# Products of blocks 1 to 3 over 64 rows in two orders of tiles, single maxima between them, first weights by GpSimd's queue

## The chip, the cores and the metric

The kernel runs on one core of a Trainium2 chip. The metric is the device time of one execution in microseconds; times of several executions are given by their median. The engines are TensorE (PE; PEld is its weight load), VectorE (DVE), ScalarE (ACT), GpSimd (POOL) and SyncE (SP), which here only issues DMA transfers. All tensors are float32.

## What is computed

The reference, cut to what matters (S = 2048 tokens, D = 640, 32 heads of width 20, one shared head of keys and values):

```python
a = x @ dft_hid_re.T;  b = x @ dft_hid_im.T
A = dft_seq_re @ a - dft_seq_im @ b            # Fourier mixing
q = (x @ wq) per head;  k = x @ wk;  v = x @ wv
p = softmax(q @ k.T * 20 ** -0.5)
B = (p @ v) of all heads @ wo
g = sigmoid((x * gate_w).sum(-1, keepdims=True))
out = g * A + (1 - g) * B
```

Every float32 factor of a product is split into a high part and a low part of type float32r, and a product is three products: high by high, high by low and low by high.

## The kernel before, in words

One long function writes the instructions of PE, ACT, DVE and POOL in the order in which they run; SP's transfers are ordered by the framework's planner, after what they depend on. It has four stages, and only the first three are touched by the change.

**Block 0** (lines 435 to 461). x is taken in four blocks of 512 tokens, each in five chunks c of 128 of the 640 features. For chunk c, `load_x1` fetches x, `move` fetches the rows of `wq`, `split_x1` and `split` make high and low parts (high on ACT, low on DVE), and PE multiplies: `kv_mm` (L397, two matmuls for keys, values and gate together, whose weights `kvg` are 41 columns wide) and, for the five tiles m of 128 columns of q, `q_mm` with its three matmuls (L119 to L121). Each tile has a PSUM bank of its own. Nine matmuls on an identity (L103) run ahead, to fill the time until data arrive. When a tile is complete, `q_out` copies its high part (ACT, L387) and low part (DVE, L388) out of PSUM into `qh` and `ql`, of which there are three buffers each, and stores both in DRAM. `kv_out` (L405 to L411) adds the two halves of the keys, splits them and copies them into six strips of `ks` by DMAs from POOL's queue; `kv_turn` (L417) transposes keys, values and gate by four small matmuls.

**Blocks 1 to 3** (lines 464 to 500). The same tiles one after the other, all five chunks of a tile in a row, with matmuls over all 128 rows of the array: 85 a block. Between the q tiles stand the first *maxima*: for a head and 128 queries the scores against 512 keys are computed on PE in a matmul over 60 rows (`a_unit`, L248; head 0 of a pair on rows 0 to 63, head 1 on rows 64 to 127) and reduced to their maximum on DVE (L255). A *unit* is both heads. They come in groups of four matmuls (two units), 13 groups in all: after tiles 2 to 4 of block 1 and after each tile of blocks 2 and 3, in the banks S1 to S4. Unit 4 is the first that reads queries of block 1, units 8, 16 and 24 the first that read keys of blocks 1, 2 and 3. The queries that the maxima read lie in `qs`, with high, high and low part of a head in three strips; `load_qs0` loads the first pair of heads from DRAM, half by half.

**The lead** (lines 1101 to 1123). 120 steps of the first product of the Fourier mixing (`y_put`, L793): each step is a pair of matmuls over 64 rows, one on the upper and one on the lower half of the array, into two banks that `lrot` hands out and that ACT evicts every 15 steps (L830). Between them the maxima go on until 80 halves are done, from step `LATE` on, in the banks S2 to S4; with unit 31 a pair of heads is complete. Then `a_reduce` to `a_final` (L258 to L278) form the maxima's rows, which SP stores to `m_d` and loads into two rows of `qs` at delays counted by `tick`. Four score matmuls of the second kind (`b_unit`, L973, over 62 rows, with ACT's exponential, L981), which need those rows, are placed by `EARLY_B` in bank V.

**The loop** (from line 1125). Hand-written plans of maxima, scores, exponentials, value products and Fourier products until the end.

## Time and profile before

| what | us |
|---|---|
| median of 3 runs | 1717.25 (1717.0 to 1718.81) |
| the profiled execution's own time | 1717.17 |
| its span, first to last instruction | 1715.4 |
| granted TensorE clock | 1.000 |

The profile is one execution. Its page gives busy times, the chain that ended last and groups of instructions; the timeline gives instructions in order of time, as "start, duration, engine, line, operation, out<-in, shape, count", with the idle time before and what ended it in brackets. A duration of a matmul covers its whole pipeline; the distance of starts is what it takes from the array. Where several equal instructions follow one another, a row merges them and its duration covers all ("x4").

### The profile page before, as it was taken

How to read it: one execution, taken by the hardware profiler on the slowest of the kernel's cores; microseconds unless marked ns; L12 is line 12 of the kernel's file. 1: busy time of each engine (PE TensorE's matmuls, PEld its weight loads, DVE VectorE, ACT ScalarE, POOL GpSimd, SP SyncE). 2: the span in 40 equal slices, each digit the busy share in tenths (PEclk: the TensorE clock that was granted, in tenths of full speed). 3: DMA queues.
4: the chain of work that ended last, by engine and by line, in shares of the span. 5: the costliest groups of instructions: out<-in, count | busy, mean ns of one | idle time of the engine just before them, and what ended most of it. 6: DMA issues, size and time to landing. Idle time of an engine off the chain costs nothing.

```text
span 1715.4 us, 43386 instructions
## 1 busy us (share of the span) xinstructions
PE 1705.8 (99%) x16766; PEld 1235.5 (72%) x16766; DVE 1378.8 (80%) x2295; ACT 1251.3 (73%) x2547; POOL 1116.0 (65%) x944
## 2 busy tenths in 40 slices
PE   9999999999999999999999999999999999999998
PEld 7687677777777777777777777777777777777665
DVE  5889888888888888888888888888888888888823
ACT  4247788888876777777777777777777767678897
POOL 2355556332366568758767888888887765547787
PEclk9999999999999999999999999999999999999999
DMA  8641223222264546546666776665555533143332
GB/s 283 190 138 52 76 76 105 76 79 72 80 224 160 190 155 209 160 147 215 224 216 203 236 233 224 203 185 186 176 176 165 160 111 117 52 123 112 113 91 99
DMA packets 180538, 261.47 MB, mean 152 GB/s; under 512 B 35872, under 2 KB 134688, under 8 KB 180332
## 3 DMA queue, kind: packets, MB, share of 16 engines
q1 hardware_dynamic: 179420, 257.55, 47.0%
q8 instruction: 132, 2.16, 0.5%
q0 software_dynamic: 768, 0.99, 0.3%
q14 instruction: 74, 0.61, 0.1%
q10 hardware_dynamic: 144, 0.16, 0.0%
HBM read 184.42 MB, written 76.99 MB: 152 GB/s over the span
## 4 chain that ended last, share of the span: by engine, by line
PE 98%; ACT 1%; DMA 0%; issue 0%; DVE 0%; POOL 0%; SPq 0%; DVEq 0%; ACTq 0%
PE av L985 27%; PE y_p L793 21%; PE b L973 19%; PE a L248 15%; PE ab L793 7%; PE oo L793 3%; PE q L119 1%; PE q L121 1%; PE q L120 1%; PE kv L397 1%; ACT pt L981 0%; DMA wraw<-in_wq_dram 0%; PE o L119 0%; PE o L121 0%; PE o L120 0%
## 5 line engine op out<-in xcount | busy, mean ns | idle before, releaser
L255 DVE TENSOR_REDUCE mx<-a 128x1 f32<-128x512 f32 x2048 | 1304.0, 686 | 242.9 <-PE a L248 203.3
L981 ACT ACTIVATE pt<-b 128x512 f32<-128x512 f32 x2048 | 1058.3, 624 | 345.6 <-PE a L248 267.6
L973 PE MATMUL b<-qs,ks 62*128 62x512 f32 x2048 | 758.2, 408 | 1.9 <-ACT pt L981 1.4
L248 PE MATMUL a<-ks,qs 60*128 60x512 f32 x2048 | 704.3, 407 | 0.4 <-DVE mx L255 0.4
L793 PE MATMUL y_p<-tb,ch 64*128 64x320 f32 x3584 | 618.5, 307 | 0.0
L793 PEld LDWEIGHTS y_p<-tb,ch 64*128 64x128 f32 x3584 | 504.7, 186 | 3.0
L985 PE MATMUL av<-pt,vsb 128*32 128x512 f32 x4096 | 484.9, 597 | 0.0
L973 PEld LDWEIGHTS b<-qs,ks 62*128 62x128 f32 x2048 | 346.2, 184 | 185.9 <-DVE mx L255 125.2
L793 PE MATMUL y_p<-tb,cl 64*128 64x320 f32 x1792 | 455.2, 306 | 0.0
L248 PEld LDWEIGHTS a<-ks,qs 60*128 60x128 f32 x2048 | 345.7, 185 | 13.1 <-issue 2.2
L793 PEld LDWEIGHTS y_p<-tb,cl 64*128 64x128 f32 x1792 | 296.5, 185 | 3.1
L985 PEld LDWEIGHTS av<-pt,vsb 128*32 128x32 f32 x4096 | 111.4, 109 | 240.2 <-issue 230.2
L548 POOL TENSOR_TENSOR cl<-craw,ch 128x1024 fp32r<-128x1024 f32 x112 | 268.3, 2395 | 9.0
L835 POOL TENSOR_TENSOR yt<-yt,yu 128x320 f32<-128x320 f32 x86 | 75.7, 881 | 293.5 <-ACT yu L830 260.3
L835 POOL TENSOR_TENSOR abt<-abt,abu 128x320 f32<-128x320 f32 x64 | 55.7, 870 | 193.8 <-ACT abu L830 172.8
L542 POOL TENSOR_TENSOR craw<-craw 128x1024 f32<-128x1024 f32 x64 | 153.3, 2395 | 0.0
L547 POOL CAST ch<-craw 128x1024 fp32r<-128x1024 f32 x112 | 116.4, 1039 | 6.4 <-PE ab L793 2.2
L793 PE MATMUL oo<-wo,osp 64*128 64x320 f32 x816 | 91.4, 306 | 0.0
L793 PEld LDWEIGHTS oo<-wo,osp 64*128 64x128 f32 x816 | 86.5, 185 | 1.6
L574 POOL TENSOR_TENSOR tb<-braw,tb 128x320 fp32r<-128x320 f32 x80 | 69.6, 875 | 0.0
L793 PE MATMUL ab<-wbh,xh 64*128 64x320 f32 x256 | 60.1, 307 | 0.0
L793 PE MATMUL ab<-wbh,xl 64*128 64x320 f32 x256 | 59.6, 305 | 0.0
(142 smaller groups left out, 1619.2 us busy)
## 6 DMA issues: line engine op xcount, KB each, us to landing
craw<-in_cre_dram SPq DMA_DIRECT2D x80, 512.0 KB
craw<-in_cim_dram SPq DMA_DIRECT2D x64, 512.0 KB
s_d<-craw SPq DMA_DIRECT2D x32, 512.0 KB
craw<-s_d SPq DMA_DIRECT2D x32, 512.0 KB
braw<-b_d SPq DMA_DIRECT2D x80, 160.0 KB
xraw<-in_xT_dram SPq DMA_DIRECT2D x32, 320.0 KB
b_d<-abt SPq DMA_DIRECT2D x64, 160.0 KB
t_d<-braw SPq DMA_DIRECT2D x64, 160.0 KB
```

Source lines behind the costliest of these rows:

```text
L119: nc.tensor.matmul(ps, wh, xh, start=(i == 0), stop=False)
L248: nc.tensor.matmul(ps, qs[v][b : b + 60, qb * P : (qb + 1) * P], ks[b : b + 60, c * ROW : (c + 1) * ROW], start=True, stop=True,)
L255: nc.vector.tensor_reduce(mx[v][:, hh, qb, c : c + 1], ps, axis=AX.X, op=ALU.max)
L542: nc.gpsimd.tensor_tensor(x, raw[0], x, op=how)
L547: nc.gpsimd.tensor_copy(h, x)
L548: nc.gpsimd.tensor_tensor(l, x, h.bitcast(F32), op=ALU.subtract)
L574: nc.gpsimd.tensor_tensor(t[:, 1], raw, t[:, 0].bitcast(F32), op=ALU.subtract)
L793: nc.tensor.matmul(ps, w, x, start=start, stop=stop)
L835: nc.gpsimd.tensor_tensor(t0, t0, t1, op=ALU.add)
L973: nc.tensor.matmul(ps, ks[b : b + 62, kc * P : (kc + 1) * P], qs[NPAIR * (qc // 2) + p][b : b + 62, (qc % 2) * ROW : (qc % 2 + 1) * ROW], ...
L981: nc.scalar.activation(t, ps, AF.Exp, scale=SCALE)
L985: nc.tensor.matmul(ps[32 * g : 32 * g + 32, :], vsb[:, kc, :], t, start=first, stop=last)
```

## The change

In blocks 1 to 3 every product over 128 rows becomes two over 64, on the upper and the lower half of the array. A new class `Tile` holds a tile's list of matmuls, takes its bank when first run, and runs the list once on each half, into the same bank. The two halves go through a block's six tiles in different orders, (kv, 1, 0, 2, 3, 4) and (0, kv, 3, 4, 1, 2), so that they are never at the same tile at one time; the second pass over a tile begins with the matmul that ended the first (its list runs backwards there), and between the passes ACT copies one column of that matmul's weights onto itself, which orders the second pass behind the first. Five banks serve these tiles. Maxima stand singly in each half's order, 30 in each, every seven matmuls from 40 on and every six from 220 on (counted over the three blocks), the lower half's four matmuls later, in the banks S2 to S4. Loads, splits and transposes are tied to positions of that count.

Block 0 keeps full matmuls, but in chunk 0 the order is changed, the products for keys and values come a chunk later, and q's tiles end one after the other. The first chunk of `wq` comes in two pieces of 256 and 384 columns by POOL's queue; `kvg` is fetched and split after chunk 1. Low parts of x from block 1 on are made by POOL. `q_out` fills the first pair of heads of `qs` from SBUF by six DMAs of POOL's queue for blocks 0 and 1, and `load_qs0` goes. In the lead, `lrot` gives other banks (the last group sits in V and F1), maxima start at step 4 rather than 8 and are 20 halves rather than 28, the four b halves stand at steps 64 to 94 rather than 102 to 117, and the maxima's rows are stored at once and loaded a tick later. One warming matmul less is made.

```diff
-    for _ in range(9):
+    for _ in range(8):
...
     def later(n, f, *args):
-        todo.append((clock["n"] + n, f, args))
+        if n < 0:
+            f(*args)
+        else:
+            todo.append((clock["n"] + n, f, args))
...
-            later(1, move, m_d[v][i].rearrange("r g t -> g r t"), m3[:, 1 + i])
+            later(1 if stage["loop"] else -1, move, m_d[v][i].rearrange("r g t -> g r t"), m3[:, 1 + i])
...
-            later(5 if stage["loop"] else 3, move, qs[v][r : r + 2], ...
+            later(5 if stage["loop"] else 1, move, qs[v][r : r + 2], ...
...
+        pieces = (slice(0, 2 * P), slice(2 * P, D))
+        raw0 = w1.tile([P, D], F32, name="wraw", bufs=2)
+        for cs in pieces:
+            nc.gpsimd.dma_start(raw0[:, cs], wq_v[:, 0, cs])
...
-                nc.vector.tensor_tensor(xl[:, c], xs[n, c], xh[:, c].bitcast(F32), op=ALU.subtract)
+                low = nc.gpsimd if n else nc.vector
+                low.tensor_tensor(xl[:, c], xs[n, c], xh[:, c].bitcast(F32), op=ALU.subtract)
...
+            def run(self, rows, i):
+                if self.ps is None:
+                    self.ops = self.ops()
+                    self.ps = rots[0](self.name)
+                if rows is not None and self.made >= self.n:
+                    i = self.n - 1 - i
+                m, w, x = self.ops[i]
+                end = self.n if rows is None else 2 * self.n
+                self.made += 1
+                r = slice(0, P) if rows is None else RG[rows]
+                nc.tensor.matmul(self.ps[:m], w[r], x[r], start=self.made == 1, stop=self.made == end)
+                if self.made == end:
+                    self.out(self.ps)
+                elif self.made == end - self.n:
+                    nc.scalar.activation(w[:, :1], words(w[:, :1]), AF.Copy)
...
+            if m == 0 and n < 2:
+                if n == 0:
+                    qs[0] = qbuf[0]
+                for hh in range(2):
+                    for k, src in enumerate((qh, qh, ql)):
+                        b = 64 * hh + 20 * k
+                        nc.gpsimd.dma_start(words(qs[0][b : b + 20, ts]), words(src[hh * DH : (hh + 1) * DH]))
...
+        load_x1(0, 0)
+        split_x1(0, 0)
+        for cs in pieces:
+            split(raw0[:, cs], wqh[:, 0, cs], wql[:, 0, cs])
+        for c in range(1, KC):
+            load_x1(0, c)
+            raw = raw_tile([P, D], "wraw") if c in (2, 3) else w1.tile([P, D], F32, name="wraw", bufs=2)
+            move(raw, wq_v[:, c])
+            if c == 1:
+                move(kvg, wkvg.rearrange("(c p) n -> p c n", p=P))
+            split_x1(0, c)
+            split(raw, wqh[:, c], wql[:, c])
+            if c == 1:
...
+            kv = [(tkv, i) for i in range(max(0, 2 * c - 2), 2 * c + 2 if c == KC - 1 else 2 * c)]
+            for t, i in kv[:2] + ops[:6] + kv[2:] + ops[6:]:
+                t.run(None, i)
...
+        rots[0] = Rot(["F1", "V", "S0", "F0", "S1"])
...
+        slots = [40 + 7 * k for k in range(24)] + [220 + 6 * k for k in range(6)]
...
+            ts = [kv_tile(n)] + [q_tile(n, m) for m in (1, 0, 2, 3, 4)]
+            for r, x in enumerate((range(6), (2, 0, 4, 5, 1, 3))):
...
+        for both in zip(*rows, strict=True):
+            for f, args in at.pop(both[0][0], ()):
+                f(*args)
+            for r, (k, t, i) in enumerate(both):
+                if t is None:
+                    a_half(r, arot.tags[arot.n % 3])
+                    arot.n += 1
+                else:
+                    t.run(r, i)
...
-    lrot = Rot(["B", "F", "B", "F"])
+    lrot = Rot(["S1", "F0", "S0", "F1"] * 3 + ["S1", "F0", "V", "F1"])
...
-    LATE = 8
-    EARLY_B = {102: (0, 0), 107: (1, 0), 112: (0, 1), 117: (1, 1)}
+    LATE = 4
+    EARLY_B = {64: (0, 0), 74: (1, 0), 84: (0, 1), 94: (1, 1)}
```

More of the change, by code (lines that the diff above doesn't have):

```diff
@@ L151, in load_qs @@
             move(t[b + 40 : b + 60], ql_d[r, ts])
-    def load_qs0(n):
-        if n == 0:
-            qs[0] = qbuf[0]
-        ts = slice(n * ROW, (n + 1) * ROW)
-        for hh in range(2):
-            r = slice(hh * DH, (hh + 1) * DH)
-            for k, src in enumerate((qh_d, qh_d, ql_d)):
-                b = 64 * hh + 20 * k
-                move(qs[0][b : b + 20, ts], src[r, ts])
     mxr = [qsp.tile([P, 32], F32, name=f"mxr{i}") for i in range(2)]
@@ L390, in q_out @@
             move(ql_d[ms, ts], ql)
-        def kv_mm(ps, n, c):
-            xh, xl = xsp[n]
-            end = c == KC - 1
-            for high in (not end, end):
-                m, x = (105, xh) if high else (41, xl)
-                nc.tensor.matmul(ps[:m], kvgs[:, c, :m], x[:, c], start=(c == 0 and high), stop=(end and high))
+            if m == 0 and n < 2:
[5 more added lines that the diff above has]
+                        nc.gpsimd.dma_start(words(qs[0][b : b + 20, ts]), words(src[hh * DH : (hh + 1) * DH]))
         def kv_out(ps, n):
@@ L448 @@
                 )
-            split_x1(0, c)
-            split(raw, wqh[:, c], wql[:, c])
-            kv_mm(pkv, 0, c)
-            for m in range(KC):
-                q_mm(pq[m], 0, m, c)
-        for c in range(KC):
-            load_x1(1, c)
-        for c in range(KC):
-            split_x1(1, c)
-        kvT = kv_out(pkv, 0)
-        for m in range(KC):
-            q_out(pq[m], 0, m)
+        rots = [rot]
+        tkv = kv_tile(0)
+        tq = [q_tile(0, m) for m in range(KC)]
+        order = [[(k, m) for m in range(KC) for k in range(3)] for c in range(KC)]
@@ new lines, with event @@
+        rots[0] = Rot(["F1", "V", "S0", "F0", "S1"])
+        at = {}
+        def event(k, f, *args):
+            at.setdefault(k, []).append((f, args))
+        NB = 17 * KC
+        for n in range(1, 4):
+            s0 = (n - 1) * NB
+            for c in range(KC):
+                if n == 1:
+                    event(s0, load_x1, 3, c)
+                if n < 3:
+                    event(s0 + 12 + 14 * c, split_x1, n + 1, c)
+            if n > 1:
+                event(s0, lambda n=n: load_w(n - 2, 0, x1.tile([P, KC, ROW], F32, tag="xr", name="wraw")))
+                event(s0 + 40, split_w, n - 2)
+            event(s0 + 50, kv_turn, n)
@@ new lines @@
+        s0 = 2 * NB
+        for k in range(2):
+            event(s0 + 25, load_x, k)
+            event(s0 + 55 + 15 * k, split_x, k)
+        event(s0 + 70, load_x, 2)
+        event(32, kv_turn, 0)
+        event(s0 + 50, gate_out)
+        slots = [40 + 7 * k for k in range(24)] + [220 + 6 * k for k in range(6)]
+        rows = [], []
+        for n in range(1, 4):
+            ts = [kv_tile(n)] + [q_tile(n, m) for m in (1, 0, 2, 3, 4)]
+            for r, x in enumerate((range(6), (2, 0, 4, 5, 1, 3))):
+                k = NB * (n - 1)
+                for t, i in [(ts[z], i) for z in x for i in range(ts[z].n)]:
+                    if k - 4 * r in slots:
+                        rows[r].append((k, None, r))
+                    rows[r].append((k, t, i))
+                    k += 1
@@ L503 @@
+        for both in zip(*rows, strict=True):
[7 more added lines that the diff above has]
+                    t.run(r, i)
+        assert not at
     abp = ctx.enter_context(tc.tile_pool(name="abp", bufs=1))
```

83 lines of the change are left out of this document (33 added, 50 removed).

## The prediction

> **What bounds the kernel now.** I read the page's busy times and its chain first, then the timeline of PE through the first 127 us, where all the edited code runs. The loop after it keeps its instructions.
>
> ```profile
> PE 1705.8 (99%) x16766; PEld 1235.5 (72%) x16766; DVE 1378.8 (80%) x2295; ACT 1251.3 (73%) x2547; POOL 1116.0 (65%) x944
> PE 98%; ACT 1%; DMA 0%; issue 0%; DVE 0%; POOL 0%; SPq 0%; DVEq 0%; ACTq 0%
> 10.63 0.40 PE L397 MATMUL kv<-xh,kvgs 128*105 128x512 f32 x1
> 26.49 0.40 PE L397 MATMUL kv<-xh,kvgs 128*105 128x512 f32 x1
> 97.80 0.31 PE L793 MATMUL ab<-w0h,xh 64*128 64x320 f32 x2
> 99.41 0.31 PE L793 MATMUL ab<-wbl,xh 64*128 64x320 f32 x2
> 122.50 0.50 PE L973 MATMUL b<-qs,ks 62*128 62x512 f32 x1 [0.34 <-ACT abt L830]
> 126.44 0.42 PE L973 MATMUL b<-qs,ks 62*128 62x512 f32 x2
> 126.67 0.42 PE L248 MATMUL a<-ks,qs 60*128 60x512 f32 x2
> ```
>
> TensorE is the chain, so a microsecond counts where PE starts its work late, pauses, or changes its form. From 10.63 to 26.49 lie four chunks of 17 matmuls: 15.86 / 68 = 0.2332 us is the **pitch** of a matmul over 128 rows and 512 columns, overlapped with its neighbours. Two matmuls over 64 rows, one on each half of the array, share a pitch: pair b to pair a is 126.67 - 126.44 = 0.23. For 320 columns a pair takes (99.41 - 97.80) / 11 = 0.1464. So halves cost nothing in themselves: 510 of them are the 255 full matmuls of today. Three stages follow from the rows: block 0 to 26.49, blocks 1 to 3 from there to 97.80 (71.31 us), the lead to 122.50 (24.70 us).
>
> **Blocks 1 to 3.** Work today: 255 matmuls and 26 pairs of maxima, 281 x 0.2332 = 65.53. Left over: 5.78.
>
> ```profile
> 92.55 0.40 PE L121 MATMUL q<-xh,wql 128*128 128x512 f32 x1
> 92.87 0.74 PE L248 MATMUL a<-ks,qs 60*128 60x512 f32 x4
> 93.54 0.50 PE L119 MATMUL q<-xh,wqh 128*128 128x512 f32 x1
> 93.88 0.39 PE L120 MATMUL q<-xl,wqh 128*128 128x512 f32 x1
> 39.40 0.31 PE L417 MATMUL kvt<-ident,kvT 41*128 41x41 f32 x2
> 40.29 0.50 PE L119 MATMUL q<-xh,wqh 128*128 128x512 f32 x1
> ```
>
> From 92.55 to 93.88 is 1.33 for four pitches (0.93): each group of four maxima costs 0.40 because the array goes from 128 rows to 60 and back. Thirteen groups make 5.2. Four transposes ahead of a group add 0.22 (40.29 - 39.40 = 0.89 against 93.54 - 92.87 = 0.67). The change keeps the array in halves from the start of block 1 on: the 5.2 shrink to one change, 0.2. It makes 60 maxima here rather than 52, so the work is 285 x 0.2332 = 66.46, with 4 x 0.22 = 0.88 for the transposes: 67.5 without waits.
>
> New waits come in its place; I price four.
>
> ```profile
> 22.53 0.40 PE L397 MATMUL kv<-xl,kvgs 128*41 128x512 f32 x1
> 28.43 0.60 ACT L387 ACTIVATE qh<-q 128x512 fp32r<-128x512 f32 x1 [1.67 <-DMA qh_d<-qh]
> 25.79 0.73 POOL L411 DMA_DIRECT2D ks<-kh  x1 [21.60 <-ACT qh L387]
> 28.52 0.51 POOL L411 DMA_DIRECT2D ks<-kh  x1
> DMA to landing us min/median/max: 1.8/3.6/5.4
> 2.01 0.22 ACT L105 ACTIVATE gate<-ident 128x16 f32<-128x16 f32 x1
> ```
>
> (a) The 12 transfers that filled qs from DRAM leave SP's queue, which costs nothing. But q tiles leave through three qh buffers; the fourth of block 0 already waits for a store today (28.43). Now GpSimd's six copies of m = 0 into qs hold the first buffer too, at 0.5 us each behind one another. Count from the first matmul of block 0's last chunk (22.53 today): q's first tile ends on the fifth matmul, its qh is done at about 2.0, the copies are issued from 2.2 on, the fifth from 4.25, landing (1.8 to 5.4, I take 3.4, as those of that window are slow) at 7.65; ACT then needs two qh (1.2) and the new one-column copy (0.2), with the x splits of block 2 queued behind. For that copy waits kv's second half, due on PE at 19 + 15 pitches and a change, 8.1. So about 1.0 lost; bounds 0 and 3.0. (b) The maxima of unit 4 need block 1's copies in qs; from the end of block 1's kv tile, POOL issues six ks copies until about 5.9, a low part (1.3) until 7.2, then these, the third at 8.4, landing near 11.2 (10.2 to 13.8). q's tile ends 15 ops (3.5) after kv's and its unit 4 is due 29 ops and four maxima later (7.7), at 11.2: 0.2 lost, bounds 0 and 2.6.
>
> ```profile
> L340 POOL TENSOR_TENSOR xl<-xraw,xh 128x640 fp32r<-128x640 f32 x6 | 9.4, 1569 | 5.7 <-ACT xh L339 5.7
> L376 DVE TENSOR_TENSOR xl<-xr,xh 128x512 fp32r<-128x512 f32 x20 | 14.7, 752 | 0.8 <-ACT xh L375 0.8
> L388 DVE TENSOR_TENSOR ql<-q,qh 128x512 fp32r<-128x512 f32 x20 | 13.6, 688 | 15.8 <-ACT qh L387 14.2 <-DMA ql_d<-ql 1.6
> L408 DVE TENSOR_TENSOR kl<-kvT,kh 20x512 fp32r<-20x512 f32 x4 | 2.7, 679 | 2.8 <-ACT kh L407 2.8
> 49.70 2.47 DVE L255 TENSOR_REDUCE mx<-a 128x1 f32<-128x512 f32 x4
> ```
>
> (c) DVE. It gives 15 low parts of x to POOL (15 x 0.752), where one costs about 1.569 x 512/640 = 1.3, hidden behind the four or more us between uses. Its dense stretch is ops 40 to 208: 168 + 24 pitches, 44.8 us. In it: 48 maxima at 2.47/4 = 0.62, nine ql at 0.69, four kv steps at 0.68: 38.7, and two waits of 0.7 for kh: 40. It fits, but unevenly: at the end of a kv tile DVE stands until about 3.2 us after the tile, and with three banks the third maximum after it is due at 3.0 and gets its bank at 3.9. That is 0.9, once, in block 2; bounds 0 and 3. (d) Unit 24 reads block 3's ks.
>
> ```profile
> 51.18 0.39 PE L397 MATMUL kv<-xh,kvgs 128*105 128x512 f32 x1
> 53.87 0.51 POOL L411 DMA_DIRECT2D ks<-kh  x1 [15.46 <-ACT kh L407]
> 55.08 1.00 POOL L411 DMA_DIRECT2D ks<-kh  x2
> ```
>
> From tile to first copy is 2.7, to the third 3.9 (55.08), plus landing: 5.7 at the least, 7.5 at the median, due 26 ops and two maxima after the tile, 28 pitches or 6.5. I take 0.4, nearer the least, since fewer other transfers run there; bounds 0 and 2.8. Sum of the stage: 67.5 + 1.0 + 0.2 + 0.9 + 0.4 = 70.0, a gain of 1.3. The 18 one-column copies (0.22 each, as the small ACT operation at 2.01) lie in ACT's idle time; without that cover they would cost as in (a).
>
> **The lead.** Work today: 120 pairs of 0.1464, 14 pairs of maxima, four b halves: 17.57 + 3.26 + 0.47 = 21.3; 3.4 is waiting.
>
> ```profile
> 98.62 10.25 DVE L255 TENSOR_REDUCE mx<-a 128x1 f32<-128x512 f32 x16
> 99.96 0.50 PE L248 MATMUL a<-ks,qs 60*128 60x512 f32 x1 [0.24 <-DVE mx L255]
> 119.81 0.49 PE L973 MATMUL b<-qs,ks 62*128 62x512 f32 x1 [0.67 <-ACT pt L981]
> 107.73 0.40 PE L248 MATMUL a<-ks,qs 60*128 60x512 f32 x1
> 111.14 1.28 SPq L111 DMA_DIRECT2D m_d<-m  x2
> 114.56 0.55 SPq L111 DMA_DIRECT2D qs<-m_d  x2
> ```
>
> DVE enters with four maxima in hand and works 10.25 us without a pause; PE waits for it (99.96). At the end the b halves, five steps apart, wait for ACT, and the loop's first b waits for the eviction of S1. After the change 20 maxima remain, so 17.57 + 2.33 + 0.47 = 20.4; b halves are ten steps apart (1.7 us against an exp of 0.6 behind an eviction), and the last group sits in V and F1, so S1 is free. What is late next is the first b, moved from step 102 to 64: it reads the maxima's rows in qs. Head 0's last maximum stands at 107.73 today (step 56), its store at 111.14, its load at 114.56, which lands, I estimate, 1.1 later: 7.9 us. Without the tick and the x load ahead of the store that is some 7.1 (bounds 6 and 8.5). That maximum is now at step 28, and 36 pairs and six maxima later is 5.27 + 0.70 = 5.97: PE waits 1.1 (0 to 2.5). With 0.6 for the rest (ACT behind evictions, V): 22.1, a gain of 2.6.
>
> **The start.**
>
> ```profile
> 1.64 0.52 SPq L111 DMA_DIRECT2D wraw<-in_wq_dram  x1
> 4.30 0.63 ACT L375 ACTIVATE xh<-xr 128x512 fp32r<-128x512 f32 x1 [2.07 <-DMA xr<-in_xT_dram]
> 5.84 0.74 ACT L114 ACTIVATE wqh<-wraw 128x640 fp32r<-128x640 f32 x1 [0.91 <-DMA wraw<-in_wq_dram]
> 11.00 0.83 DVE L115 TENSOR_TENSOR wql<-wraw,wqh 128x640 fp32r<-128x640 f32 x1 [0.34 <-ACT wqh L114]
> 5.26 0.37 DVE L446 TENSOR_TENSOR kvgs<-kvg,kvgs 128x205 fp32r<-128x205 f32 x1
> ```
>
> 85 pitches end at 26.49, so block 0 runs as if begun at 6.67. With the first weights in two pieces on POOL from 1.4, ACT has xh at 4.93 and the first piece at about 5.35; PE begins at 5.4 if it landed by then (the landings of ks, 1.8 to 5.4, would give 3.2 to 6.8). Chunk 0 is now 15 matmuls and ends at 8.9. Chunk 1 opens with kv, and kvgs now stands on DVE behind wql of chunk 1: that w lands at 7.2 to 7.6, ACT 0.74, wql 0.83, kvgs twice 0.37, so 9.6 to 10. Then 70 pitches: 26.1, a gain of 0.4 (bounds -2.7 and 1.3). One warming matmul less costs nothing: PE is idle between the last and the first product. The Trainium skill ("DMA: Bandwidth & Descriptors", section on issuing engines) says that DMAs of all issuing engines share the same 16 DMA engines, so another queue saves issue time alone; by that rule the start gains at most the 0.52 that wraw takes on SP, and if the shared engines take that back too, the sum is 0.4 higher, 1713.3, inside my range; the trace of before has no early transfer on POOL that could settle it.
>
> **Sum** for the profiled execution, 1717.17 (span 1715.4, 1.77 around it; the median of the runs is 1717.25): 0.4 + 1.3 + 2.6 = 4.3, so 1712.9. About 0.2%, 3.4 us, is what a measurement can tell from no change.
>
> **Rivals.**
> 1. *The waits take back the blocks' gain*: (a) to (d) at 2.0, 1.0, 1.3, 1.2, thus 5.5 for 2.5; 1715.9. For it: the three buffers already stop ACT today, and landings spread to 5.4. Against it: the median landing is 3.6.
> 2. *The first weights come late*: if POOL's time for a descriptor goes with rows (0.5 us for 20), 128 rows take 3.2 us a piece, the second lands near 9.5, and block 0 ends 2.7 later than today: 1717.17 + 2.7 - 3.9 = 1716.0. Against it: 0.73 and 0.51 for the same 20 rows look like a fixed price. This is also the case in which that edit doesn't do what it says.
> 3. *Slower: DVE becomes the bound.* If maxima never run close together (0.686 rather than 0.62) and each of 15 ql and 6 kv steps finds DVE waiting 0.7 for ACT, DVE needs 60 x 0.69 + 15 x 1.39 + 6 x 1.4 + 2.6 = 73, of which 2.8 lie before op 40 (9.3 us): 9.3 + 70 = 79.5, 9.5 more than my 70.0: 1722.4. It decides once DVE's share of 8 pitches (1.87 us) with two maxima passes 0.5 us. Against it: today's waits of DVE fall where it has nothing queued.
> 4. *No wait appears*: start 1.3, blocks 67.5, lead 20.8: gains of 1.3, 3.8, 3.9; 1708.2.
>
> **Numbers.** Forecast 0.54 (own range 1710 to 1715.5; about 0.42 of it under 1713.8, the 0.2% bound), rival 1 0.16, rival 2 0.09, rival 3 0.09, rival 4 0.12. Faster 0.42 + 0.12 = 0.54, same 0.12 + 0.16 + 0.09 = 0.37, slower 0.09. The range 1707.8 to 1718.0 leaves out rival 3 and edges of the others.
>
> **What would show it.** Right: no 0.3 us gaps around maxima in the blocks, a block stage near 70, a lead near 22. PE waiting for an ACT copy about 15 pitches into block 1 shows (a); a wait of b on a DMA at step 64 shows the lead's term; maxima waiting for DVE in block 2 show (c). Wrong: pairs of halves at over 0.2332, or a loop after the lead that is not the same length (1715.4 - 122.5).

## The result and the profile after

The changed kernel takes 1731.57 us (median of 6 runs, 1730.28 to 1734.88) where the kernel before takes 1717.47 (1717.0 to 1718.81): a ratio of 1.0083, with a 95% interval of 1.0073 to 1.0094. It is slower by 14.1 us; the forecast was 1712.9 and the range ended at 1718.0.

The profiled execution was the slowest of the six (1734.88). The same kernel was therefore profiled a second time, as run e8_again (1731.98). The stages, cut at the same instructions as in the prediction (first product of block 1, first `ab` product, the loop's first `b` product), in us:

| | before | forecast | after | e8_again |
|---|---|---|---|---|
| block 1 starts | 26.49 | 26.1 | 31.46 | 31.35 |
| blocks 1 to 3 | 71.31 | 70.0 | 85.84 | 82.10 |
| lead | 24.70 | 22.1 | 21.98 | 22.86 |
| loop to the end | 1592.88 | 1592.9 | 1593.65 | 1593.79 |
| span | 1715.4 | 1711.1 | 1732.9 | 1730.1 |

Of the 14.7 us by which e8_again's span is longer, the start holds 4.9 and the blocks 10.8; the lead gives back 1.8, the loop takes 0.9 more.

The busy times and the chain on the page of after hardly show it. TensorE is busier than before, and still 99%:

```profile
PE 1709.8 (99%) x17019; PEld 1250.4 (72%) x17019; DVE 1374.1 (79%) x2281; ACT 1254.0 (72%) x2566; POOL 1142.6 (66%) x973
PE 95%; DMA 2%; DVE 1%; ACT 1%; issue 0%; POOL 0%; SPq 0%; DVEq 0%; ACTq 0%
```

What shows it is PE's share of the chain (98% before, 95% now), and then the waits of PE. Here are the first six rows of the view of waits of e8_again for its first 140 us, where the kernel before waited 3.4 us in all:

```profile
PE a L241 <- DVE mx L248: 7.0, 6, 2.1
PE kv L406 <- DVE kvgs L488: 3.1, 1, 3.1
PE kv L406 <- ACT kvgs L410: 2.3, 1, 2.3
PE q L406 <- DVE ql L423: 1.4, 1, 1.4
PE warm L103 <- POOL ident masks.py:199: 1.3, 1, 1.3
PE q L406 <- ACT wqh L114: 1.3, 1, 1.3
```

The columns are us in total, times, and the longest. The places are in the timeline of PE in the trace of after (start, duration, instruction, idle time and what ended it):

```profile
6.67 1.22 PE L406 MATMUL q<-xh,wqh 128*128 128x512 f32 x2 [1.54 <-ACT wqh L114]
15.00 0.45 PE L406 MATMUL kv<-xh,kvgs 128*105 128x512 f32 x1 [2.73 <-DVE kvgs L488]
38.69 0.75 PE L406 MATMUL kv<-xh,kvgs 64*105 64x512 f32 x1 [3.28 <-ACT kvgs L410]
65.34 0.79 PE L241 MATMUL a<-ks,qs 60*128 60x512 f32 x1 [2.20 <-DVE mx L248]
74.31 0.50 PE L241 MATMUL a<-ks,qs 60*128 60x512 f32 x1 [0.59 <-DVE mx L248]
77.38 0.49 PE L406 MATMUL q<-xh,wqh 64*128 64x512 f32 x1 [1.40 <-DVE ql L423]
104.72 0.47 PE L241 MATMUL a<-ks,qs 60*128 60x512 f32 x1 [0.26 <-DMA ks<-kh]
108.53 0.49 PE L241 MATMUL a<-ks,qs 60*128 60x512 f32 x1 [1.92 <-DVE mx L248]
129.30 0.49 PE L1028 MATMUL b<-qs,ks 62*128 62x512 f32 x1 [0.86 <-DMA qs<-m_d]
```

Three of the nine (38.69, 65.34 and 74.31) end when ACT or VectorE comes to an instruction that stood in its queue, not when something slow is done; what the waits of 77.38 and 108.53 are for, e14_slots and e4_gate tell below. The row of 38.69 is read one step back, in the timeline of ACT in the same trace: the one-column copy that orders kv's second half takes 0.19 us, and stands behind a `qh` copy that waited 2.08 us for a store to give its buffer back.

```profile
37.95 0.60 ACT L422 ACTIVATE qh<-q 128x512 fp32r<-128x512 f32 x1 [2.08 <-DMA qh_d<-qh]
38.44 0.19 ACT L410 ACTIVATE kvgs<-kvgs 128x1 fp32r<-128x1 f32 x1
```

And a wait can cost more than its own length. These are the products behind the wait of 38.69 in after, and behind the same wait in e8_again (PE's timeline, products of the upper and lower half in turn; only those of kv are shown):

```profile
39.24 0.63 PE L406 MATMUL kv<-xl,kvgs 64*41 64x512 f32 x1
39.67 0.63 PE L406 MATMUL kv<-xl,kvgs 64*41 64x512 f32 x1
40.09 0.63 PE L406 MATMUL kv<-xh,kvgs 64*105 64x512 f32 x1
```

```profile
37.86 0.39 PE L406 MATMUL kv<-xl,kvgs 64*41 64x512 f32 x1
38.10 0.39 PE L406 MATMUL kv<-xl,kvgs 64*41 64x512 f32 x1
38.33 0.39 PE L406 MATMUL kv<-xh,kvgs 64*105 64x512 f32 x1
```

Starts are 0.43 us apart in the first and 0.23 in the second. In after some 13 pitches went at the slow rate, a loss of about 2.6 us (13 x 0.2). The granted clock in the trace says the same: in the blocks of after it is 0.5 from 37.66 to 44.48, from 64.97 to 68.38 and from 109.34 to 112.75, 13.6 us in all; in those of e8_again only from 105.27 to 108.68, 3.4 us. PE's waits in the blocks add up to 9.7 us in both, so the difference between the two profiles of one kernel, 85.84 against 82.10 us, is this rate.

### The profile page after: what moved, and what is told of

The parts are those of the page before. It is cut to its first block, busy times and chain, and to the rows that moved or that the text cites. A ratio compares the mean times of both kernels' runs of the same rounds, so it can differ in the third digit from the quotient of the medians.

```text
span 1732.9 us, 43923 instructions
## 1 busy us (share of the span) xinstructions
PE 1709.8 (99%) x17019; PEld 1250.4 (72%) x17019; DVE 1374.1 (79%) x2281; ACT 1254.0 (72%) x2566; POOL 1142.6 (66%) x973
## 4 chain that ended last, share of the span: by engine, by line
PE 95%; DMA 2%; DVE 1%; ACT 1%; issue 0%; POOL 0%; SPq 0%; DVEq 0%; ACTq 0%
PE av L1040 27%; PE y_p L848 21%; PE b L1028 18%; PE a L241 15%; PE ab L848 7%; PE oo L848 3%; PE q L406 3%; ACT pt L1036 1%; DMA qh_d<-qh 1%; PE kv L406 1%; DMA wraw<-in_wq_dram 0%; DVE mx L248 0%; DMA ql_d<-ql 0%; DMA xr<-in_xT_dram 0%; DVE ql L423 0%
## 5 line engine op out<-in xcount | busy, mean ns | idle before, releaser
L241 PE MATMUL a<-ks,qs 60*128 60x512 f32 x2048 | 716.1, 406 | 5.8 <-DVE mx L248 5.4
L241 PEld LDWEIGHTS a<-ks,qs 60*128 60x128 f32 x2048 | 351.3, 185 | 18.0 <-DVE mx L248 8.5
L890 POOL TENSOR_TENSOR yt<-yt,yu 128x320 f32<-128x320 f32 x86 | 75.8, 881 | 293.0 <-ACT yu L885 245.7
L406 PE MATMUL q<-xh,wqh 64*128 64x512 f32 (+1 forms) x175 | 58.7, 420 | 2.9 <-ACT wqh L114 1.5
```

The costliest lines, as they stand in the source:

```text
L241: nc.tensor.matmul(ps, qs[v][b : b + 60, qb * P : (qb + 1) * P], ks[b : b + 60, c * ROW : (c + 1) * ROW], start=True, stop=True,)
L406: nc.tensor.matmul(self.ps[:m], w[r], x[r], start=self.made == 1, stop=self.made == end)
L890: nc.gpsimd.tensor_tensor(t0, t0, t1, op=ALU.add)
```

## The experiments

All times of single runs stand beside the kernel before on the same chip, 1717.0 to 1718.2 us. The changed kernel's own six runs span 1730.28 to 1734.88, so a single total inside that span (e1_name, e4_gate) or just under it (e2_sync) tells nothing by itself; the stages and the waits do. A theory or rival with a letter is one of the run's own expectation.

**e1_name.** The first weights' ring gets a name of its own, so that chunk 1's weights no longer share it.

```diff
-        raw0 = w1.tile([P, D], F32, name="wraw", bufs=2)
+        raw0 = w1.tile([P, D], F32, name="wraw0", bufs=1)
...
-            raw = raw_tile([P, D], "wraw") if c in (2, 3) else w1.tile([P, D], F32, name="wraw", bufs=2)
+            raw = raw_tile([P, D], "wraw") if c in (2, 3) else w1.tile([P, D], F32, name="wraw", bufs=1)
```

> The changed kernel with the first chunk of wq in a tile of its own name, so that chunk 1's weights no longer share its ring; this puts the transfer of chunk 1's weights third on SP instead of tenth. Block 1 starts at 31.46 in the changed kernel (26.49 before). Theory A, order on SP: chunk 1's weights, landed at 12.5, come by 9, PE opens chunk 1 at the end of chunk 0 (12.3) rather than at 15.0, block 1 starts near 28.8, total 2.5 to 3 us less. Theory B, the DMA engines are shared with POOL's pieces and everything there is late: block 1 starts at 30.5 or later.

Measured: 1733.35 us. The wait of 2.7 us for `kvgs` at 15.00 is gone, so the order on SP was its cause; but the first piece now lands at 7.05 (6.18 in after), the first product comes at 7.54 rather than 6.67, the products run 0.43 us apart until 13.6, and block 1 starts at 30.28, only 1.1 earlier than in e8_again. Blocks 84.35: the 1.1 did not reach the end.

**e2_sync.** The two pieces of the first weights go by SP's queue.

```diff
-            nc.gpsimd.dma_start(raw0[:, cs], wq_v[:, 0, cs])
+            move(raw0[:, cs], wq_v[:, 0, cs])
```

> The changed kernel with the two first pieces of wq by SP's queue instead of POOL's, first on SP. Theory A (POOL's queue brings the pieces late, at 6.15 and 8.1, PE stands 1.5 us and then runs at a pitch of 0.43): PE begins at 5.3 to 5.6 with a pitch of 0.233 from the start, block 1 starts at 26 to 27, 4.5 to 5.5 us less in all. Theory C, the new order within chunk 0 and the late kvgs are what costs: block 1 starts at 29 or later.

Measured: 1730.04 us. Block 1 starts at 28.53, 2.8 earlier than in e8_again, with no wait for `kvgs`. Of these 2.8 the lead sees 0.8 (112.69 against 113.45), because kv's second half now waits longer, as PE's timeline shows:

```profile
37.11 0.75 PE L406 MATMUL kv<-xh,kvgs 64*105 64x512 f32 x1 [4.63 <-ACT kvgs L410]
```

It begins at 37.1 here and at 37.55 in e8_again: a nearly fixed time, whatever the start.

**e3_dram.** `qs[0]` is filled from `qh_d` and `ql_d` by SP as before the change (`load_qs0`, at the end of block 0 and at step 41), not by POOL from the `qh` buffers.

```diff
-                        nc.gpsimd.dma_start(words(qs[0][b : b + 20, ts]), words(src[hh * DH : (hh + 1) * DH]))
...
+        event(41, load_qs0, 1)
```

> The changed kernel with the first pair of qs filled from DRAM on SP as before, so that POOL's six copies no longer hold the first qh buffer. Theory A (those copies keep ACT from the one-column copy for which PE waits 3.3 us at 38.69): that wait falls under 1.0, the stretch of 0.43 pitches behind it goes too, blocks 1 to 3 take about 80.5 instead of 85.8; unit 4 may wait up to 1.5. Theory D, the stores on SP hold the buffers: the wait stays over 2.5 and the blocks stay within 1.5 us of 85.8.

Measured: 1725.31 us, the largest gain of one edit: blocks 77.84. Kv's second half no longer waits; the first maxima wait 0.4 for `qs<-ql_d`, at 41.25. POOL's six copies did hold the buffers, at a price of some 4 us (82.10 - 77.84) by single profiles, of which e3_dram has 6.8 us at half rate in its blocks and e8_again 3.4.

**e4_gate.** The gate's operations move from step 220 to the end of the blocks.

```diff
-        event(s0 + 50, gate_out)
...
         assert not at
+        gate_out()
```

> The changed kernel with the five gate operations issued after block 3 instead of at position 220. Theory A (two of them, 0.17 us each before, took 1.89 and 1.29 on DVE and ended when GpSimd's operation ended, and maxima stood behind them): PE's wait of 2.07 at 108.5 and the 0.43 pitches behind it go, blocks 82 to 82.5 instead of 85.8, the lead at most 0.5 longer. Theory E, DVE is late there from the maxima themselves: the wait stays over 1.5.

Measured: 1731.0 us. In after, two operations of VectorE on 128x16 words take 1.89 and 1.29 us where they took 0.17 before; the timelines of DVE and POOL show the first beside a POOL operation, and both end at 105.6 (the second ends at 107.88, beside one of POOL that ends at 107.85):

```profile
103.72 1.89 DVE L465 TENSOR_SCALAR gz<-gz 128x16 f32<-128x16 f32 x1
```

```profile
103.33 2.25 POOL L199 TENSOR_TENSOR w1l<-wraw,w1h 128x960 fp32r<-128x960 f32 x1
```

With the gate away, the wait of 1.92 at 108.53 is gone, yet the blocks take 82.07, as e8_again's 82.10: kv's second half waited 3.4 instead of 2.3, with 6.8 us at half rate from 36.8 on, and a later maximum 1.8 instead of 1.1.

**e5_lead.** The kernel before with the changed lead alone.

```diff
-    lrot = Rot(["B", "F", "B", "F"])
+    lrot = Rot(["S1", "F0", "S0", "F1"] * 3 + ["S1", "F0", "V", "F1"])
...
-    LATE = 8
-    EARLY_B = {102: (0, 0), 107: (1, 0), 112: (0, 1), 117: (1, 1)}
+    LATE = 4
+    EARLY_B = {64: (0, 0), 74: (1, 0), 84: (0, 1), 94: (1, 1)}
```

(with the two changed delays of `later`.)

> The kernel before with the changed kernel's lead alone (order of the lead's banks, transfers of m_d issued at once, first b-products at steps 64 to 94). In the changed kernel's profile the stretch from the first ab-product to the loop's first b-product took 21.98 us against 24.70 before. Theory A (the lead's gain is its own, the loss is all ahead of it): the lead starts at 97.8 as before, takes 22.0, the rest 1592.9 to 1593.7; time 1714.5 to 1715.5 where before is 1717.2. Rival B (the lead is only short because the changed blocks hand over an empty vector queue and loaded weights): 24 to 25 us, time 1716.8 to 1718.

Measured: 1725.39 us (1724.6 to 1725.79, 5 runs), ratio 1.0045 with an interval of 1.0032 to 1.0059. Neither theory: the lead starts at 99.27, 1.5 later than before, because its first product waits for a maximum (its first bank is now S1, which the blocks of the kernel before use for maxima), and it takes 30.8 us. PE's timeline has one more wait, which is followed by products at half rate (granted clock 0.5 from 112.84 to 123.08):

```profile
116.76 0.79 PE L976 MATMUL b<-qs,ks 62*128 62x512 f32 x1 [6.16 <-DMA qs<-m_d]
```

The first b at step 64 needs the maxima's rows. A pair of heads has 64 maxima; 52 are done when this lead begins and 60 when the changed kernel's begins. So the last of the 64 starts 9.2 us into this lead (108.49) and 4.4 us into e8_again's (117.82), and the first b follows it by 8.3 and 8.5 us. What shortened the changed lead is that 8 of the 28 maxima products had moved into the blocks. The lead's gain was lent by the blocks.

**e6_four.** The edits of e2_sync, e3_dram and e4_gate together, and `load_w` 12 steps later.

```diff
-                event(s0, lambda n=n: load_w(n - 2, 0, x1.tile([P, KC, ROW], F32, tag="xr", name="wraw")))
+                event(s0 + 12, lambda n=n: load_w(n - 2, 0, x1.tile([P, KC, ROW], F32, tag="xr", name="wraw")))
```

> The changed kernel with four edits undone or moved together: the first weights' pieces on the sync queue, qs[0] filled from qh_d and ql_d, the gate's operations behind block 3, the weights of the loop's first operand loaded 12 steps into blocks 2 and 3. Theory A (each loss was a wait of TensorE at its own place, with some us at half speed behind it): block 1 starts at 28.5 as with the sync queue alone; the 77.84 us of the blocks with qs[0] from DRAM lose the 1.99 us wait of the gate and its slow products (1.5) and the 0.74 us at the start of block 2, which leaves 73.0 to 74.5; lead 22.4; time 1717.5 to 1720. Rival B (products over 64 rows in two orders are slow in themselves, waits or not): blocks stay at 77 or more, time 1721.5 or more.

Measured: 1723.97 us. Block 1 starts at 28.02, but the blocks stay at 77.65. Theory A fails in its number: the waits do not add. Kv's second half waits again (2.97 at 34.93), although POOL holds no buffer now. ACT's timeline:

```profile
32.95 0.60 ACT L432 ACTIVATE qh<-q 128x512 fp32r<-128x512 f32 x1 [4.17 <-DMA qh_d<-qh]
34.19 0.60 ACT L432 ACTIVATE qh<-q 128x512 fp32r<-128x512 f32 x1 [0.64 <-DMA qh_d<-qh]
34.68 0.19 ACT L420 ACTIVATE kvgs<-kvgs 128x1 fp32r<-128x1 f32 x1
```

In e3_dram the same copies stand at 32.73, 33.97 and 34.47. The stores give buffers back at a time of their own, and the later start of e3_dram had hidden it. Part of that time is made by the edit itself: SP issues nothing from 28.9 to 32.9 here, and what it issues next is the load of `qs` from `qh_d`, which stands in its queue ahead of block 0's later stores (from 30.6 to 32.7 in e3_dram). The changed kernel has no such load.

**e7_filled.** e6_four with 12 warming products for 8.

```diff
-    for _ in range(8):
+    for _ in range(12):
```

> As e6_four, with 12 warming products where that has 8, so that TensorE has work in the 1.9 us ahead of its first product of weights. Theory A (it is the idle time that halves the rate of the products behind it): the first products run at a pitch near 0.23 us from the start, block 1 begins 1.2 to 1.8 us earlier than in e6_four, 26.7 to 27.4, and the time falls by as much. Rival B (the first products are slow because their weights or x land and are split late): the pitch of some 0.4 us stays, block 1 begins within 0.3 us of e6_four. Rival C (the warming products end too late and hold the first product up): first product later than 7.1, no gain.

Measured: 1727.93 us. The first half of theory A holds: no slow product at the start, block 1 at 27.01, 1.0 earlier. The trace's record of the granted clock begins, at 1.0, at 6.65 us here, ahead of the first product, and at 9.61 in e6_four. PE's timeline of e7_filled:

```profile
6.89 0.73 PE L416 MATMUL q<-xh,wqh 128*128 128x512 f32 x2
7.46 0.63 PE L416 MATMUL q<-xl,wqh 128*128 128x512 f32 x2
7.92 0.86 PE L416 MATMUL q<-xh,wqh 128*128 128x512 f32 x3
```

The second half does not: kv's second half still begins at 35.1 (e6_four: 34.93), after a wait of 4.14, and then some 13 pitches at half rate (granted clock 0.5 until 40.79). The start's gain came back as a loss of 4.

**e8_again.** The changed kernel unaltered.

> The changed kernel itself, profiled a second time, since its profile was of its slowest execution (1734.88 against a median of 1731.57). Theory A (the waits belong to the kernel): the same waits at the same places, 3.0 to 3.6 us ahead of the second half of kv in block 1, 2 us at the start of block 2, 1.5 us on ql in block 2, 2 us in block 3 beside the gate's operations; blocks 82 to 86 us, time 1730.3 to 1732.5. Rival B (some of them were of that one execution): one or more is missing or under half as long.

Measured: 1731.98 us. The longer waits of after are all there, if not in size, and the first is smaller than theory A had it: 2.25 for 3.28 at kv's second half, 1.84 for 2.20 at block 2's start, 1.41 on `ql`, 2.05 beside the gate; and one of 1.10 at the start of block 3 that after does not have. The rate behind them is what differs. PE's timeline of e8_again:

```profile
37.55 0.47 PE L406 MATMUL kv<-xh,kvgs 64*105 64x512 f32 x1 [2.25 <-ACT kvgs L410]
61.90 0.49 PE L241 MATMUL a<-ks,qs 60*128 60x512 f32 x1 [1.84 <-DVE mx L248]
72.55 0.50 PE L406 MATMUL q<-xh,wqh 64*128 64x512 f32 x1 [1.41 <-DVE ql L423]
88.64 0.49 PE L241 MATMUL a<-ks,qs 60*128 60x512 f32 x1 [1.10 <-DVE mx L248]
104.68 0.49 PE L241 MATMUL a<-ks,qs 60*128 60x512 f32 x1 [2.05 <-DVE mx L248]
```

**e9_touch.** e6_four, with the one-column copies of kv and q_1_0 on POOL and the x splits 10 to 14 steps later.

```diff
-                    nc.scalar.activation(w[:, :1], words(w[:, :1]), AF.Copy)
+                    if m == P and self.name != "q_1_0":
+                        nc.scalar.activation(w[:, :1], words(w[:, :1]), AF.Copy)
+                    else:
+                        nc.gpsimd.tensor_copy(w[:, :1], words(w[:, :1]))
...
-                    event(s0 + 12 + 14 * c, split_x1, n + 1, c)
+                    event(s0 + 26 + 13 * c, split_x1, n + 1, c)
```

> As e6_four, where the copy that orders a tile's second half behind its first is made by GpSimd for the kv tiles and q_1_0 (ScalarE keeps the others), and the splits of the next block's x come 14 steps later so that GpSimd is free for it. In e6_four TensorE waited 3.10 us at kv's second half in block 1 (34.93), for a ScalarE copy of 0.19 us that stood behind qh copies waiting for stores. Theory A (it is the queue of ScalarE, not the store as such, that holds TensorE): that wait and the slow products behind it go, blocks 72 to 74.5 where e6_four had 77.65, block 1 starts at 28.0, time 1718.5 to 1721. Rival B (the stores themselves hold the blocks, through qh and ql buffers and PSUM banks): the wait comes back within block 1 at the next tile that needs a bank, blocks 76 or more.

Measured: 1724.11 us, blocks 77.83 where e6_four had 77.65. The wait at kv's second half is down to 0.3, at 31.70, so ACT's queue did hold it; the next thing that needs the stores then waits, the first maxima in PE's timeline:

```profile
40.94 0.46 PE L251 MATMUL a<-ks,qs 60*128 60x512 f32 x1 [3.09 <-DMA qs<-ql_d]
```

Rival B, at another place than it named: the stores hold the blocks, now through the loads of `qs` from DRAM, which come after them (SP issues nothing from 28.6 to 32.6 here), and the first maxima cannot come before about 41. The changed kernel itself, which fills `qs` from SBUF, waits 0.2 us at most for its first maxima.

**e10_spread and e11_ends.** Other orders of tiles, one tile split in two runs on the lower half, so that a block's tiles end at its steps 25, 45, 60, 75, 85 and 85; the banks are handed out by a list. e10_spread stands on e9_touch (with `load_qs0(1)` at step 46 for 41), e11_ends on the changed kernel.

```diff
-            for r, x in enumerate((range(6), (2, 0, 4, 5, 1, 3))):
+            seqs = [(kv, up[:10], 1), (a, up, 1), (b, up, 1), (c, up, 1), (d, down[10:] + up[5:], 1), (e, down, 0)], [
+                (e, up, 1), (kv, down[5:], 0), (d, up[:5], 1), (a, down, 0), (b, down, 0), (c, down, 0), (d, down[:10], 0)]
```

> As e9_touch, with other orders of tiles for the two halves: the tiles of a block end at its steps 25, 45, 60, 75, 85 and 85, where the changed kernel's end at 25, 40, 70, 70, 85 and 85. In e6_four TensorE waited at 57.74 (1.14) and 84.65 (1.44) for maxima that stood behind two ql subtractions in a row, the second of them waiting for a qh buffer and its store. Theory A (tiles that end in pairs bunch the copies and stores): those two waits go, the ones at the end of kv in block 2 (0.7 and 1.6) stay; blocks 69 to 72, time 1715 to 1718. Rival B (VectorE's work beside the blocks is the limit, whatever the order): blocks within 1 us of e9_touch.

> The changed kernel with the other orders of tiles alone (ends at 25, 45, 60, 75, 85, 85). Theory A: the start and the wait at kv's second half in block 1 stay (block 1 from 31.4, wait 2 to 3.5), the waits at 52 to 55 and 88 to 92 go, blocks 78 to 81 against 82 to 86, time 1726.5 to 1729.5. Rival B (the order of ends has no part): blocks 82 to 86, time 1730 to 1732.

Measured: 1726.54 and 1737.84 us, both slower than their base (blocks 78.70 and 87.38; of e11_ends's blocks 13.6 us went at half rate, so its loss is in part that). The wait of 1.4 on `ql` in block 2 is gone in both, but the last two tiles still end together at step 85, and now the lead's first product waits for them (1.99 in PE's timeline of e10_spread), and a maximum at the start of block 3 waits 2.1 and 2.2:

```profile
107.30 0.47 PE L858 MATMUL ab<-w0h,xh 64*128 64x320 f32 x2 [1.99 <-DVE ql L434]
```

Spread this way, the ends are no remedy; what another order could do is not told by it.

**e12_best.** e10_spread with 12 warming products.

> As e10_spread with 12 warming products instead of 8. Theory A: the first products run at full rate, block 1 starts 1.0 us earlier than in e10_spread (27.0), nothing gives it back since no wait is left at kv's second half; time 0.7 to 1.2 below e10_spread, 1714 to 1717, which would be at or below the kernel before. Rival B (as from e6_four to e7_filled, where the block began 1.0 earlier and waited 1.2 longer): no gain over e10_spread.

Measured: 1726.84 us (1726.17 to 1727.49, 5 runs), ratio 1.0052, interval 1.0039 to 1.0066. Block 1 starts 1.15 earlier (27.45) and the first maxima wait until 41.38, the same time as in e10_spread (3.6 us, put down to `ks<-kh`). Rival B.

**e13_loads.** e9_touch, with x of blocks 2 and 3 loaded later.

```diff
-        for c in range(KC):
-            load_x1(2, c)
...
-                    event(s0, load_x1, 3, c)
+                    event(s0 + 14, load_x1, 2, c)
+                    event(s0 + 50, load_x1, 3, c)
```

> As e9_touch, with x of block 2 loaded from step 14 of block 1 on and x of block 3 from step 50 on (2.6 MB that e9_touch issues ahead of, or among, the stores of block 0's q). Theory A (transfers that nobody needs yet stand in front of the stores and of qs[0]): ScalarE's qh copies no longer wait for stores near 30 to 34 us, the wait of 3.24 us for qs at the first maxima (40.94) falls under 1 us, blocks 73.5 to 75.5 where e9_touch had 77.83, time 1719 to 1722. Rival B (the maxima's banks and VectorE set the pace from 41 us on, wherever the first one starts): the later waits on VectorE grow by as much, blocks within 1 us of 77.8.

Measured: 1722.05 us, blocks 74.14, but block 1 starts at 29.84, 2.4 later: the first products of this run went at half rate until 13.1, in PE's timeline (in e9_touch, with the same eight warming products, they ran at full rate from the first one):

```profile
7.11 1.22 PE L416 MATMUL q<-xh,wqh 128*128 128x512 f32 x2 [1.98 <-ACT wqh L114]
8.13 1.05 PE L416 MATMUL q<-xl,wqh 128*128 128x512 f32 x2
8.98 1.48 PE L416 MATMUL q<-xh,wqh 128*128 128x512 f32 x3
10.26 1.05 PE L416 MATMUL q<-xh,wql 128*128 128x512 f32 x2
```

Three products in 1.28 us (8.98 to 10.26): 0.43 each, on all 128 rows. The first maxima stand at 41.36 still (40.94 in e9_touch). The lead starts at 103.98, 1.3 earlier than in e9_touch; the rest of the shorter blocks is the later start, so the run does not tell the theories apart.

**e14_slots.** e13_loads, with two pairs of maxima moved away from the end of kv in block 2.

```diff
-        slots = [40 + 7 * k for k in range(24)] + [220 + 6 * k for k in range(6)]
+        slots = [40 + 7 * k for k in range(24) if k not in (10, 11)] + [207, 213] + [220 + 6 * k for k in range(6)]
```

> As e13_loads, with the two pairs of maxima at steps 110 and 117, beside the end of kv in block 2, moved to steps 207 and 213 of block 3, where none stood. In e9_touch TensorE waited 0.74 (65.22) and 1.56 (68.28) there, for VectorE, which stood idle on ScalarE's kh (0.7) and then had five maxima ahead of ql. Theory A (the order of VectorE's queue): both waits go, with 0.5 to 1.5 us of slow products, blocks 2.3 to 3.8 shorter than e13_loads. Rival B (VectorE is bound as a whole there): the waits move to the next maxima, blocks within 1 us of e13_loads.

Measured: 1721.95 us, blocks 73.77, within 0.4 of e13_loads as rival B has it. The wait of 0.6 for the maximum is gone, the one on `ql` is not:

```profile
65.17 0.49 PE L416 MATMUL q<-xh,wqh 64*128 64x512 f32 x1 [1.46 <-DVE ql L436]
```

No maximum stands ahead of that `ql` now. DVE and ACT have it at 64.42 and 63.79, right after the tile's last product: what PE waits for is the bank of the tile that has just ended, because the five banks go round in turn (with the banks of e10_spread's list this wait is gone). The other wait of this run is at the end of block 2, in the timelines of ACT, DVE and PE:

```profile
80.45 0.60 ACT L435 ACTIVATE qh<-q 128x512 fp32r<-128x512 f32 x1 [2.46 <-DMA qh_d<-qh]
```

```profile
81.08 0.69 DVE L436 TENSOR_TENSOR ql<-q,qh 128x512 fp32r<-128x512 f32 x1 [2.36 <-ACT qh L435]
81.68 2.48 DVE L258 TENSOR_REDUCE mx<-a 128x1 f32<-128x512 f32 x4
```

```profile
82.42 0.49 PE L251 MATMUL a<-ks,qs 60*128 60x512 f32 x1 [2.28 <-DVE mx L258]
```

A store holds a `qh` buffer, ACT waits for the buffer, VectorE for ACT, four maxima that are ready stand behind VectorE's `ql`, and PE waits for their banks. The DMA view from 74 to 82, in slices of 0.2 us, shows how full the transfers were from 75.8 on: four stores each of `qh` and `ql`, 256 KB apiece, and the 800 KB of `load_w`.

```profile
GB/s 0 0 0 0 58 133 38 32 109 269 352 371 378 378 371 384 378 390 415 392 439 364 425 343 326 435 318 328 379 420 358 399 420 389 389 379 399 389 328 297
```

**e15_fill.** e14_slots with 12 warming products.

> As e14_slots with 12 warming products instead of 8: first products at full rate, block 1 starts 0.5 to 1.2 us earlier, about 27.0. Theory A: as no transfer holds the first maxima any more, the gain reaches the end: time 0.5 to 1.2 below e14_slots, 1715 to 1719. Rival B: it is given back at the first maxima (41 us), as in e7_filled and e12_best: same time as e14_slots.

Measured: 1723.96 us (1721.96 to 1725.06, 6 runs), ratio 1.0034, interval 1.0022 to 1.0047. Block 1 starts at 26.86, 3.3 earlier than in e14_slots, and the lead at 104.13 (e14_slots: 103.96): all of it was lost, 3.0 at the first maxima, which began at 40.23. Rival B, clearly. SP is idle here too ahead of the load of `qs` from `qh_d`, from 28.0 to 31.6.

**e16_few and e17_fewk.** e15_fill with 26 pairs of maxima from step 58 on and the lead of before; in e17_fewk `kl` is made by POOL.

```diff
-        slots = [40 + 7 * k for k in range(24) if k not in (10, 11)] + [207, 213] + [220 + 6 * k for k in range(6)]
+        slots = [58 + 7 * k for k in range(26) if k not in (7, 8)] + [240, 247]
...
-            nc.vector.tensor_tensor(kl, kvT[:DH], kh.bitcast(F32), op=ALU.subtract)
+            nc.gpsimd.tensor_tensor(kl, kvT[:DH], kh.bitcast(F32), op=ALU.subtract)
```

(the second pair of lines in e17_fewk alone.)

> As e15_fill, with 26 pairs of maxima in blocks 1 to 3 instead of 30, the first at step 58 instead of 40, and the lead of before (14 pairs of maxima, its banks, first b at step 102). Block 1 starts at 26.9. Theory A (the blocks waited because the maxima began ahead of their operand and came faster than VectorE, with three banks, takes them): first maxima at 40.4 without a wait, blocks 67.5 to 70.5 us, so the lead starts at 94.5 to 97.5 (97.80 before, 104.13 in e15_fill) and takes 24.5 to 25.5; time 1714 to 1717.5. Rival B (the order over 64 rows with its pairs of ends is what waits): waits of 3 to 5 us stay in the blocks, the lead starts at 99 or later, time 1719 or more.

> As e16_few, with kl subtracted by GpSimd, so that VectorE neither works on it (0.68 us, four times) nor stands idle for kh ahead of it (0.7 us). Theory A: the waits on VectorE at the ends of kv go, 0.5 to 1.5 us less than e16_few, time 1713.5 to 1717, at or below the kernel before. Rival B (VectorE had the room already with 26 pairs): same time as e16_few within 0.5 us.

Measured: 1723.07 us, and 1724.1 (1723.63 to 1725.03, 5 runs; ratio 1.004, interval 1.0026 to 1.0053). The first maxima no longer wait, as theory A has it; the lead starts at 103.25 and 104.38 all the same, which is rival B's side. The chain of e14_slots stands at the start of block 3, in PE's timeline of e16_few:

```profile
77.61 0.49 PE L248 MATMUL a<-ks,qs 60*128 60x512 f32 x1 [2.07 <-DVE mx L255]
```

and the granted clock is 0.5 from 78.97 to 82.38. With the lead of before, 14 pairs of maxima in it, the lead takes 24.20 and 24.17 us again: e5_lead's reading, from the other side. Beside e15_fill, e16_few's blocks are 1.2 us shorter (76.1 for 77.3) and its lead 2.0 longer (24.2 for 22.2), so by these two profiles the four pairs cost the blocks little more than their work on PE, 0.93. No version was faster than the kernel before.

## Why the prediction was wrong

**What was right.** Pairs of halves keep the pitch: 0.23 us between pairs in the quiet stretches (37.86, 38.10, 38.33 above). The work of the blocks was forecast at 67.5 us without waits; e14_slots's 73.77, none of it at half rate, less its waits of 4.5 leaves 69.3, and 1.7 of these stand right beside its five pauses, some 0.3 apiece beyond their length. The groups' change of form did go: ten pairs take 2.33 us in the quiet stretch of e14_slots, with or without maxima among them. In the waits, (d) was 0.4 and came as 0.3, (b) was 0.2 and came as 0.5 in e8_again (not at all in after), and (c) came at its place, 0.6 for 0.9. The first b on `m_d` waited 0.9 for 1.1, and the lead took 22.0 to 22.9 for 22.1.

**The start: forecast 0.4 gained, 4.9 lost.** Rival 2 had the direction. The step that failed is "w lands at 7.2 to 7.6". The pieces on POOL land at 6.2 and 8.1, where the first was forecast at 5.35; chunk 1's weights, which share their ring, go out tenth on SP, and ACT can take them only at 12.57, so that `kvgs` is late (e2_sync gives 2.8 back). A second step left a term out: "One warming matmul less costs nothing". In after the warming products start 0.21 us apart to the last, and so do the first products of q at 0.43 until about 10.4; in the kernel before the warming products themselves go from 0.21 to 0.12 at 4.5, so that the work begins at the full rate. Filling the time with 12 of them gives 1.0 back (e7_filled beside e6_four); whether the one product that was taken away makes the difference, or the longer pause behind it (1.5 for 0.7), was not run. Another 0.5 is scatter of that rate: e2_sync, where it fell again from 8.3 to 11.7, starts block 1 that much later than e6_four, with the same start. The rest, 0.5, is a first product at 6.9 where the kernel before has 5.8.

**The blocks: forecast 1.3 gained, 10.8 lost.** In e8_again they hold 9.7 us of waits and 3.4 us at half rate, which cost 1.7; the 70.7 that remain are less than the 71.3 of before, where PE waited for nothing. So the loss is waits and what follows them, and the step that failed is the list of four waits. (a) was sized at 1.0, inside bounds of 0 to 3.0, and measured 2.25 and 3.28. The wait was right in kind, but its cause was only partly POOL's copies (e3_dram): the stores of block 0's q run while all transfers together move up to 390 GB/s (30 to 32 us in e6_four and e9_touch), and kv's second half, or in the kernels that fill `qs` from DRAM the first maxima, wait for them at a nearly fixed time, 35 to 38 or 40 to 41, whatever the start (e2_sync, e6_four, e7_filled, e9_touch, e12_best, e15_fill). The forecast counted it from the end of block 0, as if it moved with it. Not in the list at all were: the same chain at the ends of blocks 1 and 2, where two tiles end together and their stores meet `load_w` (1.84 and 1.10 in e8_again; that the pairing of the ends makes it is argued, and e11_ends did not bear it out); a bank that is asked for as its tile ends (1.41; e14_slots); the gate beside POOL (2.05; e4_gate). These unlisted waits make 6.4 of the 9.7 us of waiting in e8_again's blocks. And a wait was priced at its length, where several brought 3.4 or 6.8 us at half rate behind them, a loss of about 1.7 or up to 3.4 us.

**The lead: right in number, but on loan.** "The lead gains 2.6" took 20 maxima for 28 as given, and with them its mechanism held, down to the wait of the first b. e5_lead shows that the same edits without the moved maxima make the lead 6.1 us longer. So the gain is moved work, and at 0.2332 a pair, where it went, it was counted nearly right (e16_few).

**Rivals.** Rival 3 ended on the right side, with the wrong mechanism: VectorE was 79% busy in the whole, and in e14_slots it stood idle for 2.36 us at its `ql` while four maxima behind that were ready. There it is not the sum of its work that bound, but its order, behind ACT, behind a store.

**What stays open.** How the loss in the blocks divides between the pairs of ends, `load_w` and the buffers was not settled: a fourth `qh` and `ql` buffer, which would tell, wasn't tried. That the fixed time of 40 to 41 is the stores' alone is argued from the runs with different starts; e13_loads, meant to show it, was blurred by its slow start, and SP's idle time of some 4 us ahead of the load of `qs` is a rival that no run takes away.

## What to carry to other kernels

That TensorE never waits in a stage, and how busy the other engines are there, does not tell how near their queues are to holding it up: before its order is changed, follow each in-order queue, SP's too, through one period, with what stands ahead of each instruction and when the buffer that it needs comes back. If a wait stays at a fixed time when the start moves, an earlier start is worth nothing ahead of it. Try a part of a change alone as well as undone: here most of the lead's 2 us was another stage's loan.

## What the runs showed of the hardware

**The rate behind an idle time.** At the slow rate the products start 0.43 us apart instead of 0.23, on 64 and on 128 rows, and the granted clock in the trace is 0.5, for 3.4 or 6.8 us at a time (10.2 in e5_lead). In the blocks this followed every pause of 3.16 us or more (eight of eight: after, e1_name, e2_sync, e4_gate, e7_filled, e11_ends, e12_best, e17_fewk), some of those between 1.4 and 3.1 (2.20 in after at 65.34 and 1.4 in e3_dram at 67.92, but not 2.25 in e8_again at 37.55 nor 2.97 in e6_four at 34.93), and none under 1.4. The Trainium skill ("TensorE: Matmul & The Clock Gate", Part 1) says that the array falls to half its clock after an idle window of about 3.4 us, and that the window runs freely, so that one kernel differs from run to run: the pitch, the lengths of the slow stretches and the scatter agree, but pauses of 1.4 to 2.4 us did it here too.

**The rate at the start.** The first warming products run at half rate in every profile, 0.21 us apart, and the trace has no value of the granted clock until the pitch changes. With 8 warming products that is at 4.8 to 5.2 us in three profiles (e2_sync, e9_touch, e10_spread) and at 9.4 to 13.6 in the other nine; with 12 of them it is at 6.0 to 7.3 in all five (e7_filled, e12_best, e15_fill, e16_few, e17_fewk). A mean of the granted clock over such a stretch, as for 6 to 14 us of e13_loads, reads 1.00, though its products are 0.43 apart: the record begins at 13.14 there.

**VectorE beside GpSimd.** An operation of VectorE of 0.17 us took 1.89 and another 1.29 while GpSimd subtracted two tensors, and each ended with GpSimd's (after; without such company both took 0.17, in e4_gate). The Trainium skill ("GPSIMD Engine Reference", Key points) says that GpSimd shares its SBUF interfaces with VectorE, with contention when VectorE works in a mode of two ports; the trace agrees, with 1.89 for 0.17 us, though in which mode the two operations ran it does not show.
